# Residual quantizer on one core: norms as a ninth column, scores code by code, code constants in the mask product, a new order

## The chip, the cores and the metric

The kernel runs on one core of a Trainium2 chip. The metric is the device time of one execution in microseconds (us). A core has five engines that take their instructions in order, each from its own queue: PE (matrix products into PSUM), VectorE (DVE in the profile), ScalarE (ACT), GpSimd (POOL) and SyncE (SP), which here only issues DMAs.

## The reference

An audio codec's encoder and decoder around a residual vector quantizer, for x of shape 2 x 16000 x 512 in bf16, four codebooks of eight codes:

```python
z = sum(xp[:, i:i+T, :] * dw_enc[i] for i in range(3))   # 3 taps along time
z = silu(z)
res, q = z, 0
for s in range(4):
    cb = codebooks[s]                                     # 8 x 512
    d2 = (res*res).sum(-1)[..., None] - 2*res@cb.T + (cb*cb).sum(-1)
    idx = d2.argmin(-1)
    q, res = q + cb[idx], res - cb[idx]
y = sum(qp[:, i:i+T, :] * dw_dec[i] for i in range(3))
```

Everything is rounded to bf16 after each step, as JAX does; which code wins depends on these roundings.

## The kernel before

**Tiles.** Each of the two rows of 16000 frames is cut into tiles of G groups of 128 frames: 6, 8 and seven of 16 in the first row, seven of 16, 8 and 6 in the second, so 18 tiles, 14 of them large. A tile's frames lie so that the 512 features are four blocks of 128 partitions, with 128 frames of a group side by side.

**Stages of a tile.** `load` brings x in by transposing DMAs, one for each group, on SP. `front` makes the encoder: for each half of the features (h) three tap products of two blocks each (L538 to L541, on ScalarE or VectorE), two additions on VectorE (`TA`, `Z`), `exp` on ScalarE (L545), +1 on either (L547); `front2` the reciprocal on ScalarE (L557) and the gate product on VectorE. `select` scores three codebooks at once, `resid` subtracts the three chosen codes from z and scores the fourth, `back` multiplies the chosen codes with the decoder's taps and stores y.

**Scores.** `gram` (L561) fills PSUM for each group with 64 columns: 32 columns of z times z, block by block of 32 frames, of which a frame's own norm is the diagonal, and 32 columns of z times the 32 codes (times -2). Before these, one product of the identity with `MSK` (L569) puts -2^100 off the diagonal, so that a maximum over the 32 columns gives the norm (L609). L610 copies the code columns of three codebooks to `S` and adds `CC2`, the codes' own norms (of two codebooks; zero for the third).

**Decisions.** Then `select` takes the codebooks s = 0, 1, 2 in turn, all on arrays of 16 groups x 8 codes in each partition: the norm rounded to bf16 (`TR`), the score without the code's norm (`PR = S - CCF`, bf16), `V = PR + TR`, `KEY = V + CCB` in the upper half of a 32-bit word whose lower half holds the code's number, the minimum `M`, and the one-hot `OHA` by comparing (L370 is the helper that issues all of VectorE's two-input operations). For the next codebook, PE transposes the one-hot (L647), a copy `OT` brings it to SBUF (L652), and a product with `BD` gives the correction of the scores (L657), which L625 or L630 adds. The norm of the residual is the old one plus the chosen code's score: `E2 = RC * OHA`, its sum `RD` (L663), `rr[1] = rr[0] + RD[0]`, rounded into `TR[1]` (L666); for s = 1 `TR[2] = rr[1] + RD[1]`.

**Windows, residual, back.** `windows` transposes the one-hots by PE (L680) and copies them to `OHW` (L686), win0 for three codebooks, win3 for the fourth. `resid` has 24 pieces a tile: PE multiplies with `CBN` (L709), and the piece goes back to z by VectorE as an addition (L717) or by ScalarE as a copy, for which PE adds z itself first (L708, L715). `back` is PE (L766 to L770), a copy by ScalarE to one of four buffers `YB` (L774), and stores on SP (L797).

**What sets the order.** All steps of all tiles are recorded in a `Plan` with their engine, a cost, what they read and write, and a key. `Plan.order` then places them one after another: always the step that can start first by these costs, and among equals the one of lowest rank; the rank comes from tables (`WHEN`, by stage and by part of the run, and `NUDGE`, by stage and tile, empty here). `SHARE` and `SLACK` decide which of two engines takes a step that either can do. Where the plan leaves PE waiting over 1 us, it puts in `fill` products without a use (L817), which keep PE busy. The instructions are written out in that order, so each engine's queue is fixed.

Of the kernel before, what the change touches and what calls it, by code (L numbers as in the profile page):

```python
# [8 lines left out]
BF16 = mybir.dt.bfloat16  # L9
F32 = mybir.dt.float32  # L10
# [207 lines left out]
def kernel(  # L218
# [30 lines left out]
    SHARE = (18.22, 2.18, -1.48)  # L249
    SLACK = (0.8, -4.91, -0.79)  # L250
    QUOTA = {"ACT": 4, "DVE": 4}
    MARGIN = (0, 0, 0, 1)
    WHEN = {"setup": ((0.01, 1.859), (0.613, 1.215), (0.919, 1.13)), "load": ((-1.633, 0.741), (-1.622, 0.601), (-2.139, 0.741)),
            "pad": ((-1.343, 0.11), (-1.736, 0.115), (-2.291, 0.134)), "taps": ((0.214, 0.643), (-0.413, 0.648), (0.468, 1.172)),
            "exp": ((0.672, 0.12), (0.683, 0.024), (0.853, 0.023)), "plus1": ((1.084, 0.218), (0.349, 0.232), (0.344, 0.644)),
            "recip": ((0.542, 0.819), (0.604, 0.213), (1.49, 0.627)), "gate": ((-0.104, 0.84), (0.557, 0.649), (1.589, 0.937)),
            "score0": ((-0.134, 0.016), (0.889, 0), (0.11, 0)), "decide": ((1.83, 0.266), (-0.088, 0.293), (0.585, 0.224)),
            "win0": ((2.026, 0), (2.064, 0), (2.265, 0)), "resid": ((1.585, 0.742), (1.683, 0.632), (1.582, 0.974)),
            "score3": ((2.326, 1.043), (2.779, 0.347), (2.915, 1.644)), "decide3": ((1.265, 0.194), (2.773, 0.35), (3.38, 0.645)),
            "win3": ((3.143, 0.143), (2.987, 1.212), (3.452, 0.209)), "back": ((2.709, 0.604), (3.156, 1.105), (4.055, 0.674))}  # L260
    NUDGE = {}
# [25 lines left out]
    def sb(shape, dt, name):  # L287
# [7 lines left out]
    ONES = sb([P, P], BF16, "ONES")  # L295
    MSK = sb([P, NMK, ZW], BF16, "MSK")
    IDH = sb([P, HB, 1], F32, "IDH")
    CBT = sb([P, KT, NC], BF16, "CBT")
    CBM2 = sb([P, KT, NC], BF16, "CBM2")
    CCF = sb([P, 1, NC], F32, "CCF")  # L300
    CC2 = sb([P, 1, N3], F32, "CC2")
    CCB = sb([P, 1, NC], BF16, "CCB")
# [12 lines left out]
    SS = [{"S": sb([P, GM, N3], F32, f"S{b}"), "rr": sb([P, 3, GM, 1], F32, f"rr{b}"), "RD": sb([P, 2, GM, 1], F32, f"RD{b}"),  # L315
           "TR": sb([P, 3, GM, 1], BF16, f"TR{b}"), "RC": sb([P, GM, C], F32, f"RC{b}"), "PR": sb([P, GM, C], BF16, f"PR{b}"),
           "V": sb([P, GM, C], BF16, f"V{b}"), "M": sb([P, GM, 1], F32, f"M{b}"), "E2": sb([P, GM, C], F32, f"E2{b}"),
           "OT": [sb([GCM, P], BF16, f"OT{b}_{s}") for s in range(2)],
           "PR3": sb([P, GM, C], BF16, f"PR3{b}"), "rr3": sb([P, GM, 1], BF16, f"rr3{b}"),
           "V3": sb([P, GM, C], BF16, f"V3{b}"), "M3": sb([P, GM, 1], F32, f"M3{b}")} for b in range(2)]  # L320
# [51 lines left out]
    def setup():  # L372
# [7 lines left out]
        add("DVE", 0.25, key, lambda: nc.vector.tensor_reduce(out=IDH[:, :, 0], in_=IDENT.rearrange("p (q c) -> p c q", c=HB), axis=AX.X, op=ALU.add),  # L380
            ["I"], ["IDH"])
        add("DVE", 0.3, key, lambda: nc.vector.tensor_scalar(out=MSK[:, :, 0:HB], in0=IDH.rearrange("p c o -> p o c").to_broadcast([P, NMK, HB]),
            scalar1=BIG, scalar2=-BIG, op0=ALU.mult, op1=ALU.add), ["IDH"], ["MSK"])
# [49 lines left out]
        j = add("ACT", 0.2, key, lambda: nc.scalar.copy(CCF[:, 0, :], ps(bc)[:, 0:NC]), [], ["CCF"], after=[j])  # L433
        j = add("ACT", 0.2, key, lambda: nc.scalar.copy(CCB[:, 0, :], ps(bc)[:, 0:NC]), [], ["CCB"], after=[j])
        pool_memset(CC2, 0.0, ["CC2"], 0.2, ("setup", -5, 0))
        add("ACT", 0.2, key, lambda: nc.scalar.copy(CC2[:, 0, 0:2 * C], ps(bc)[:, 0:2 * C]), [], ["CC2"], free=bc, after=[j])

# [84 lines left out]
    def front(st, h):  # L522
# [12 lines left out]
        for k in range(K):  # L535
            for c in range(2):
                i = 2 * h + c
                dst, src, w = (tb if k else ta)[:, c], X[:, i, k:k + G, :].rearrange("p g c -> p (g c)"), WENC[:, k, i:i + 1]  # L538
                either({"ACT": act(R), "DVE": dve(R, 3.84) + 0.06}, key, lambda dst=dst, src=src, w=w: nc.scalar.mul(dst, src, w),  # L539
                       lambda dst=dst, src=src, w=w: nc.vector.tensor_scalar(out=dst, in0=src, scalar1=w, scalar2=None, op0=ALU.mult),  # L540
                       allx + ["WENC"], [("TB" if k else "TA", c)])  # L541
            if k == 1:
                tt(ta, ta, tb, ALU.add, dve(2 * R, 1.92), key, [("TB", 0), ("TB", 1)], [("TA", 0), ("TA", 1)])
        tt(Z, v(ta), v(tb), ALU.add, dve(2 * R, 1.92), key, [(t, c) for t in ("TA", "TB") for c in range(2)], zt)
# [16 lines left out]
    def gram(st, g0, g1, r0, r1, box):  # L561
        F, Z = ZF[st["n"] % NZ], ZB[st["n"] % NZ]
        for g in range(r0, r1):
# [4 lines left out]
            if u == 0:  # L568
                nc.tensor.matmul(o, lhsT=IDENT, rhs=MSK[:, 0:nb, :], start=True, stop=False)  # L569
# [8 lines left out]
    def products(st, g0, g1, key, reads, box):  # L578
        j = None
        for r0 in range(g0, g1, GPART):  # L580
            r1 = min(r0 + GPART, g1)
            j = add("PE", (r1 - r0) * 0.16 + 0.19 * (r0 == g0), key, lambda r0=r0, r1=r1: gram(st, g0, g1, r0, r1, box), reads, [],
                    take=("SA"[g1 - g0 > NMK], box) if j is None else None, dest="DVE" if j is None else None, after=[] if j is None else [j],
                    mm=(r1 - r0) * 16 + (r0 == g0))
# [5 lines left out]
    def select(st):  # L590
# [4 lines left out]
        S, M, V, PR, RC, E2 = W["S"][:, 0:G], W["M"][:, 0:G], W["V"][:, 0:G], W["PR"][:, 0:G], W["RC"][:, 0:G], W["E2"][:, 0:G]  # L595
        rr = [W["rr"][:, j, 0:G] for j in range(3)]
        TR = [W["TR"][:, j, 0:G] for j in range(3)]
        RD = [W["RD"][:, j, 0:G] for j in range(2)]
        A = OHA[n % NOH]
        zt = [("Z", n % NZ, i, u) for i in range(KT) for u in range(2)] + [("ZC", n % NZ)]  # L600
        nq = len(st["split"])
        for q, (g0, g1) in enumerate(st["split"]):
            box = {}
            key = ("score0", n, q / nq)
            j = products(st, g0, g1, key, zt + ["MSK", "I"], box)

            def evac(g0=g0, g1=g1, box=box):
                v = view(g0, g1, box)
                nc.vector.tensor_reduce(out=rr[0][:, g0:g1, 0], in_=v[:, :, 0:HB], axis=AX.X, op=ALU.max)  # L609
                nc.vector.tensor_tensor(out=S[:, g0:g1], in0=v[:, :, HB:HB + N3], in1=CC2.to_broadcast([P, g1 - g0, N3]), op=ALU.add)  # L610
            add("DVE", dve((g1 - g0) * (HB + N3)) + 0.07, key, evac, ["CC2"], [("S", b), ("rr", b, 0)], free=box, after=[j])
        small = dve(GC)
        tiny = dve(G)
        pbox = None
        for s in range(3):
            key = lambda f: ("decide", n, (s + f / 10) / 3)
            cs = slice(s * C, (s + 1) * C)
            if s == 0:
                add("DVE", tiny, key(0), lambda: nc.vector.tensor_copy(TR[0], rr[0]), [("rr", b, 0)], [("TR", b, 0)])
                tt(PR, S[:, :, cs], CCF[:, :, cs].to_broadcast([P, G, C]), ALU.subtract, small, key(0), [("S", b), "CCF"], [("PR", b)])  # L620
                rc, rct = S[:, :, cs], ("S", b)
            else:
                pc = lambda pbox=pbox: ps(pbox)[:, 0:GC].rearrange("p (g c) -> p g c", c=C)
                if s == 1:
                    add("DVE", small, key(0), lambda pc=pc, cs=cs: nc.vector.tensor_tensor(out=RC, in0=pc(), in1=S[:, :, cs], op=ALU.add),  # L625
                        [("S", b)], [("RC", b)], free=pbox, after=[pj])
                    tt(PR, RC, CCF[:, :, cs].to_broadcast([P, G, C]), ALU.subtract, small, key(0), [("RC", b), "CCF"], [("PR", b)])
                    rc, rct = RC, ("RC", b)
                else:
                    add("DVE", small, key(0), lambda pc=pc, cs=cs: nc.vector.tensor_tensor(out=PR, in0=pc(), in1=S[:, :, cs], op=ALU.add),  # L630
                        [("S", b)], [("PR", b)], free=pbox, after=[pj])
            tt(V, PR, TR[s].to_broadcast([P, G, C]), ALU.add, small, key(1), [("PR", b), ("TR", b, s)], [("V", b)])
            KY = KEY[0]
            k16 = KY.bitcast(BF16).rearrange("p g (c h) -> p g c h", h=2)
            tt(k16[:, 0:G, :, 1], V, CCB[:, :, cs].to_broadcast([P, G, C]), ALU.add, small, key(2), [("V", b), "CCB"], [("KEY", 0)])
# [26 lines left out]
            tt(E2, rc, OH, ALU.mult, small, key(5), [rct, ("OHA", n % NOH)], [("E2", b)])  # L662
            add("DVE", small, key(5), lambda s=s: nc.vector.tensor_reduce(out=RD[s][:, :, 0], in_=E2, axis=AX.X, op=ALU.add), [("E2", b)], [("RD", b, s)])  # L663
            if s == 0:
                tt(rr[1], rr[0], RD[0], ALU.add, tiny, key(6), [("RD", b, 0), ("rr", b, 0)], [("rr", b, 1)])
                add("DVE", tiny, key(6), lambda: nc.vector.tensor_copy(TR[1], rr[1]), [("rr", b, 1)], [("TR", b, 1)])  # L666
            else:
                tt(TR[2], rr[1], RD[1], ALU.add, tiny, key(6), [("RD", b, 1), ("rr", b, 1)], [("TR", b, 2)])
# [20 lines left out]
    def resid(st):  # L689
# [33 lines left out]
        PR3, rr3, V3, M3 = Q["PR3"][:, 0:G], Q["rr3"][:, 0:G], Q["V3"][:, 0:G], Q["M3"][:, 0:G]  # L723
# [131 lines left out]
```

## Time and profile before

| | |
|---|---|
| times of three runs, us | 720.34, 721.6, 722.49; median 721.6 |
| span of the profiled execution, us | 721.9 |
| mean granted PE clock, share of full | 0.956 |
| DMA, MB and mean GB/s | 71.89, 100 |
| fill products (L817) | 283, 74.3 us |
| residual pieces on VectorE (L717) | 131 |
| residual pieces on ScalarE (L715) | 301 |

The chain of work that ended last is by engine:

```profile
DVE 54%; PE 25%; ACT 9%; issue 7%; DMA 2%; SPq 1%; ACTq 0%; DVEq 0%
```

How to read the rows that follow: a group's row gives line, engine, operation, names and shapes (output <- input, partitions x elements), how often, then busy us and mean ns of one, then the engine's idle time just before and what ended it. A row of stretches gives the stretch, its length, and for each engine the busy us with the number of instructions, then the granted clock, the DMA share and GB/s. A row of waits gives who waited for whom: us in total, times, longest. A timeline row begins with start and duration in us.

### The profile page before, as it was taken

The numbers are of one execution on the slowest core, as the hardware profiler recorded it, in microseconds if no ns is written. First come the engines' busy times: TensorE is split into PE (matmuls) and PEld (weight loads), VectorE is DVE, ScalarE is ACT, GpSimd is POOL, SyncE is SP. The second block draws the span as 40 slices with busy tenths as digits, with TensorE's granted clock in tenths as the row PEclk, the third lists the DMA queues.
The fourth block names the chain that finished last, engine by engine and source line by source line (L and its number), as shares of the span: only waits on it lengthen the run. The fifth ranks groups of instructions, "written<-read, shape, count | busy, mean of one in ns | idle before, by whom it ended". The sixth has DMA issues, their size and how long they took to land.

```text
span 721.9 us, 24372 instructions
## 1 busy us (share of the span) xinstructions
PE 593.8 (82%) x10729; PEld 291.3 (40%) x10729; DVE 670.1 (93%) x1252; ACT 658.3 (91%) x581; POOL 7.0 (1%) x35
## 2 busy tenths in 40 slices
PE   5896686897788879888787988789878877899995
PEld 2343243344334434434343443334434433544442
DVE  8779799999999999999999999899999999999893
ACT  5878899799999999999999999999999999999766
POOL 2000000000000000000000000000000000000000
PEclk9999798999999999999899999999999999999998
DMA  5454464634164452535426274842544150112406
GB/s 112 102 96 97 95 119 96 139 72 88 29 164 81 111 106 87 127 66 162 90 79 129 46 155 96 158 88 77 124 143 75 38 130 31 62 60 90 143 8 213
DMA packets 163968, 71.89 MB, mean 100 GB/s; under 512 B 155567, under 2 KB 155599, under 8 KB 163862
## 3 DMA queue, kind: packets, MB, share of 16 engines
q1 hardware_dynamic: 163646, 69.90, 41.9%
q8 instruction: 84, 1.38, 0.8%
q10 hardware_dynamic: 216, 0.43, 0.2%
q14 instruction: 22, 0.18, 0.1%
HBM read 0.43 MB, written 32.77 MB: 46 GB/s over the span
## 4 chain that ended last, share of the span: by engine, by line
DVE 54%; PE 25%; ACT 9%; issue 7%; DMA 2%; SPq 1%; ACTq 0%; DVEq 0%
DVE ZB L717 12%; DVE ZB L370 10%; PE ps L709 8%; PE ps L708 6%; DVE TB L540 6%; PE ps L575 5%; DVE TA L370 4%; DVE TA L540 3%; DVE EX L547 3%; ACT EX L545 2%; DVE OHW L686 2%; ACT EX L557 2%; PE ps L766 2%; ACT ZB L715 2%; PE ps L817 2%
## 5 line engine op out<-in xcount | busy, mean ns | idle before, releaser
L709 PE MATMUL ps<-OHW,CBN 128*128 128x512 bf16 (+1 forms) x768 | 268.4, 386 | 17.6 <-DVE ZB L717 9.5
L715 ACT CAST ZB<-ps 128x1024 bf16<-128x1024 f32 (+2 forms) x301 | 257.1, 941 | 27.2 <-PE ps L709 25.0
L708 PE MATMUL ps<-ZB,IDENT 128*128 128x512 bf16 (+1 forms) x537 | 209.3, 390 | 29.0 <-DVE ZB L717 12.8
L717 DVE TENSOR_TENSOR ZB<-ZB,ps 128x1024 bf16<-128x1024 bf16 (+2 forms) x131 | 137.9, 1068 | 3.0 <-PE ps L709 2.1
L709 PEld LDWEIGHTS <-CBN 128*128 128x128 bf16 x768 | 75.3, 99 | 136.8 <-issue 69.9
L774 ACT CAST YB<-ps 128x1024 bf16<-128x1024 f32 x126 | 123.0, 1048 | 6.4 <-PE ps L766 3.9
L545 ACT ACTIVATE EX<-ZB 128x4096 bf16<-128x4096 bf16 (+2 forms) x36 | 115.0, 3198 | 11.4 <-DVE ZB L370 11.3
L557 ACT ACTIVATE EX<-EX 128x4096 bf16<-128x4096 bf16 (+2 forms) x36 | 114.6, 3195 | 0.2
L575 PEld LDWEIGHTS <-ZB 128*32 128x32 bf16 x8064 | 76.2, 96 | 51.1 <-issue 46.6
L575 PE MATMUL ps<-ZB 128*32 128x64 bf16 x8064 | 88.4, 198 | 8.3 <-DVE ZB L370 2.4
L540 DVE TENSOR_SCALAR TB<-XT,WENC 128x2048 bf16<-128x2048 bf16 (+2 forms) x135 | 90.5, 689 | 0.1
L817 PE MATMUL ps<-MSK,IDENT 128*128 128x512 bf16 x283 | 74.3, 410 | 11.0 <-issue 3.4
L766 PE MATMUL ps<-WDEC,OHW 128*128 128x512 bf16 x252 | 72.6, 382 | 12.1 <-DVE ZB L717 6.4
L708 PEld LDWEIGHTS <-IDENT 128*128 128x128 bf16 x537 | 53.9, 100 | 64.0 <-issue 12.5
L370 DVE TENSOR_TENSOR ZB<-ZB,EX 128x4096 bf16<-128x4096 bf16 (+2 forms) x36 | 72.6, 2017 | 3.6 <-ACT EX L557 3.5
L370 DVE TENSOR_TENSOR TA<-TA,TB 128x4096 bf16<-128x4096 bf16 (+2 forms) x36 | 72.7, 2019 | 1.2 <-ACT TB L539 0.8
L370 DVE TENSOR_TENSOR ZB<-TA,TB 128x4096 bf16<-128x4096 bf16 (+2 forms) x36 | 72.6, 2017 | 0.4
L540 DVE TENSOR_SCALAR TA<-XT,WENC 128x2048 bf16<-128x2048 bf16 (+2 forms) x71 | 47.4, 682 | 0.3
L817 PEld LDWEIGHTS <-IDENT 128*128 128x128 bf16 x283 | 27.7, 104 | 45.1 <-issue 21.4
L547 DVE TENSOR_SCALAR EX<-EX 128x4096 bf16<-128x4096 bf16 (+2 forms) x36 | 39.1, 1085 | 3.9 <-ACT EX L545 3.8
L766 PEld LDWEIGHTS <-OHW 128*128 128x128 bf16 x252 | 23.1, 98 | 39.5 <-issue 17.0
L686 DVE COPY OHW<-ps 96x1024 bf16<-96x1024 bf16 (+5 forms) x34 | 21.6, 635 | 10.3 <-PE ps L680 5.3
(100 smaller groups left out, 401.5 us busy)
## 6 DMA issues: line engine op xcount, KB each, us to landing
out_dram<-YB SPq DMA_DIRECT2D x33, 448.0 KB
out_dram<-YB SPq DMA_DIRECT2D x28, 512.0 KB
XT<-in_x_dram SPq DMA_TRANSPOSE x283
out_dram<-YB SPq DMA_DIRECT2D x30, 60.0 KB
out_dram<-YB SPq DMA_DIRECT2D x31, 2.0 KB
out_dram<-YB SPq DMA_DIRECT2D x2, 224.0 KB
YB<-in_dw_dec_dram ACTq DMA_DIRECT2D x1, 384.0 KB
out_dram<-YB SPq DMA_DIRECT2D x1, 384.0 KB
```

The costliest lines, as they stand in the source:

```text
L370: add("DVE", cost, key, lambda: nc.vector.tensor_tensor(out=out, in0=a, in1=b, op=op), reads, writes, **kw)
L540: lambda dst=dst, src=src, w=w: nc.vector.tensor_scalar(out=dst, in0=src, scalar1=w, scalar2=None, op0=ALU.mult),
L545: add("ACT", act(2 * R), ("exp", n, h), lambda: nc.scalar.activation(v(ex), Z, ACT.Exp, scale=-1.0), zt, [("EX", sl), "ACTTAB"], hold="E")
L557: nc.scalar.add_instruction(mybir.InstActivation(name=nc.get_next_instruction_name(), engine=mybir.EngineType.Activation, func=ACT.Reciprocal,
L575: nc.tensor.matmul(o[HB * q:HB * (q + 1), u * ZW:(u + 1) * ZW].rearrange("p (s c) -> p s c", s=2), lhsT=blk, rhs=both, start=False, stop=( ...
L708: nc.tensor.matmul(o, lhsT=IDENT, rhs=zg[:, k0:k0 + nk, :], start=True, stop=False)
L709: nc.tensor.matmul(o, lhsT=CBN[s, u][:, i * P:(i + 1) * P], rhs=W[:, k0:k0 + nk, PADC:PADC + P], start=not on_act, stop=True)
L715: nc.scalar.copy(zg, v)
L717: nc.vector.tensor_tensor(out=zg, in0=zg, in1=v, op=ALU.add)
L766: nc.tensor.matmul(o, lhsT=W[:, k, PADC:PADC + P], rhs=WDEC[u], start=True, stop=not wrap)
L774: add("ACT", act_psum(1024), key, lambda k=k, box=box, Y=Y, k0=k0: nc.scalar.copy(Y[:, 2 * (k - k0):2 * (k - k0) + 2, :].rearrange("p g d ...
L817: nc.tensor.matmul(PS[j // 2][:, 512 * (j % 2):512 * (j % 2) + NMK * ZW], lhsT=IDENT, rhs=MSK.rearrange("p u w -> p (u w)"), start=True, s ...
```

## The change

Four edits.

1. The frame's norm is kept as a ninth column of `E2`, beside the eight masked scores, so that one sum over nine columns gives the next norm; the separate `rr`, `RD` and their addition go.
2. `PR`, `V`, `TR`, `PR3`, `V3`, `rr3` and the constants are laid out code by code (codes outermost, groups innermost), `S`, `RC` and `KEY` group by group as before.
3. `MSK` has three more rows, in which the code norms of two codebooks stand as three bf16 parts; `TID` (32 rows of identity, three rows of ones) takes the identity's place in the mask product, which so adds the code norms. `CC2` goes, and L610's addition is a copy. The mask has 35 rows in place of 128. The fill product multiplies ones (`FB`) in place of `MSK`.
4. The tables `SHARE`, `SLACK`, `WHEN` have other numbers, and `NUDGE` has 17 rows of 18 numbers, one for each tile.

```diff
-    SHARE = (18.22, 2.18, -1.48)
-    SLACK = (0.8, -4.91, -0.79)
+    SHARE = (94.853, 2.191, 1.099)
+    SLACK = (-12.996, -111.301, -17.404)
...
-    NUDGE = {}
+    NUDGE = {"back": (3.954, -1.84, 0.016, 0.025, 0.009, 0.557, 0.035, -0.021, 0.035, 0.051, 0.006, 0.002, 0, 0.181, 0.022, 0.443, 3.888, 2.204),
...
-        add("DVE", 0.25, key, lambda: nc.vector.tensor_reduce(out=IDH[:, :, 0], in_=IDENT.rearrange("p (q c) -> p c q", c=HB), axis=AX.X, op=ALU.add),
-            ["I"], ["IDH"])
...
+        idh = IDENT[0:HB, 0:HB].rearrange("p (o c) -> p o c", o=1)
+        add("DVE", 0.2, key, lambda: nc.vector.tensor_copy(TID[0:HB], idh.to_broadcast([HB, P // HB, HB])), ["I"], ["TID"])
...
-        pool_memset(CC2, 0.0, ["CC2"], 0.2, ("setup", -5, 0))
-        add("ACT", 0.2, key, lambda: nc.scalar.copy(CC2[:, 0, 0:2 * C], ps(bc)[:, 0:2 * C]), [], ["CC2"], free=bc, after=[j])
...
+        def ccrows():
+            for q in range(NPART):
+                nc.tensor.matmul(ps(bq)[0:2 * HB, 0:NC], lhsT=EQ[:, q, :], rhs=CCD[:, q, :], start=(q == 0), stop=(q == NPART - 1))
+        j = add("PE", 0.4, key, ccrows, ["CCD", "EQ"], [], take=("S", bq), mm=NPART)
+        add("DVE", 0.2, key, lambda: nc.vector.tensor_copy(MSK[HB:KM, :, HB:HB + 2 * C], ps(bq)[HB:KM, 0:2 * C].rearrange(
+            "p (o c) -> p o c", o=1).to_broadcast([KM - HB, NMK, 2 * C])), [], ["MSK"], free=bq, after=[j])
...
-                nc.tensor.matmul(o, lhsT=IDENT, rhs=MSK[:, 0:nb, :], start=True, stop=False)
+                nc.tensor.matmul(o, lhsT=TID.rearrange("p q c -> p (q c)"), rhs=MSK[:, 0:nb, :], start=True, stop=False)
...
-                nc.vector.tensor_reduce(out=rr[0][:, g0:g1, 0], in_=v[:, :, 0:HB], axis=AX.X, op=ALU.max)
-                nc.vector.tensor_tensor(out=S[:, g0:g1], in0=v[:, :, HB:HB + N3], in1=CC2.to_broadcast([P, g1 - g0, N3]), op=ALU.add)
+                nc.vector.tensor_reduce(out=E2[0][:, g0:g1, C], in_=v[:, :, 0:HB], axis=AX.X, op=ALU.max)
+                nc.vector.tensor_copy(S[:, g0:g1], v[:, :, HB:HB + N3])
...
-                tt(PR, S[:, :, cs], CCF[:, :, cs].to_broadcast([P, G, C]), ALU.subtract, small, key(0), [("S", b), "CCF"], [("PR", b)])
+                tt(PR, swap(rc), CCF[:, cs].to_broadcast([P, C, G]), ALU.subtract, small, key(0), [rct, "CCF"], [("PR", b)])
...
-            tt(V, PR, TR[s].to_broadcast([P, G, C]), ALU.add, small, key(1), [("PR", b), ("TR", b, s)], [("V", b)])
+            tt(V, PR, TR[s].to_broadcast([P, C, G]), ALU.add, dve(GC, 1.92), key(1), [("PR", b), tr(s)], [("V", b)])
...
-            tt(k16[:, 0:G, :, 1], V, CCB[:, :, cs].to_broadcast([P, G, C]), ALU.add, small, key(2), [("V", b), "CCB"], [("KEY", 0)])
+            tt(swap(k16[:, 0:G, :, 1]), V, CCB[:, cs].to_broadcast([P, C, G]), ALU.add, small, key(2), [("V", b), "CCB"], [("KEY", 0)])
...
-            tt(E2, rc, OH, ALU.mult, small, key(5), [rct, ("OHA", n % NOH)], [("E2", b)])
-            add("DVE", small, key(5), lambda s=s: nc.vector.tensor_reduce(out=RD[s][:, :, 0], in_=E2, axis=AX.X, op=ALU.add), [("E2", b)], [("RD", b, s)])
-            if s == 0:
-                tt(rr[1], rr[0], RD[0], ALU.add, tiny, key(6), [("RD", b, 0), ("rr", b, 0)], [("rr", b, 1)])
-                add("DVE", tiny, key(6), lambda: nc.vector.tensor_copy(TR[1], rr[1]), [("rr", b, 1)], [("TR", b, 1)])
-            else:
-                tt(TR[2], rr[1], RD[1], ALU.add, tiny, key(6), [("RD", b, 1), ("rr", b, 1)], [("TR", b, 2)])
+            tt(E2[s][:, :, 0:C], rc, OH, ALU.mult, small, key(5), [rct, ("OHA", n % NOH)], [e2(s)])
+            res = E2[1][:, :, C] if s == 0 else W["RR"][:, 0:G]
+            add("DVE", dve(G * (C + 1)), key(5), lambda s=s, res=res: nc.vector.tensor_reduce(out=res, in_=E2[s], axis=AX.X, op=ALU.add),
+                [e2(s)], [e2(1) if s == 0 else ("RR", b)])
+            if s == 1:
+                add("DVE", tiny, key(6), lambda: nc.vector.tensor_copy(TR[2][:, 0, :], W["RR"][:, 0:G]), [("RR", b)], [tr(2)])
...
-                nc.vector.tensor_copy(PR3[:, g0:g1], v[:, :, HB + N3:])
+                nc.vector.tensor_copy(PR3[:, :, g0:g1], swap(v[:, :, HB + N3:]))
...
-            nc.tensor.matmul(PS[j // 2][:, 512 * (j % 2):512 * (j % 2) + NMK * ZW], lhsT=IDENT, rhs=MSK.rearrange("p u w -> p (u w)"),
-                             start=True, stop=True)
+            nc.tensor.matmul(PS[j // 2][:, 512 * (j % 2):512 * (j % 2 + 1)], lhsT=IDENT, rhs=FB, start=True, stop=True)
```

`swap` exchanges groups and codes in an access pattern; it moves nothing.

## The prediction

> **What bounds the kernel now.** I read the busy shares first, then the span in four stretches, then the waits, then the prices of single operations.
>
> ```profile
> PE 593.8 (82%) x10729; PEld 291.3 (40%) x10729; DVE 670.1 (93%) x1252; ACT 658.3 (91%) x581; POOL 7.0 (1%) x35
> ```
> ```profile
> core 0: us, PE busy (x) PEld busy (x) DVE busy (x) ACT busy (x) POOL busy (x), PEclk, DMA share, GB/s
> 0.00:60.00 60.00, 47.45 (x525) 22.29 (x526) 48.34 (x151) 44.49 (x79) 3.78 (x29) 0.94 0.49 102
> 60.00:144.00 84.00, 61.24 (x885) 28.00 (x884) 77.93 (x120) 72.90 (x55) 0.00 (x0) 0.86 0.53 110
> 144.00:648.00 504.00, 422.54 (x8207) 210.75 (x8205) 485.98 (x844) 486.93 (x387) 3.18 (x6) 0.97 0.42 95
> 648.00:722.00 74.00, 62.53 (x1117) 30.26 (x1114) 57.82 (x140) 53.93 (x62) 0.00 (x0) 0.96 0.33 114
> ```
>
> In the middle, 144 to 648 us, VectorE and ScalarE are both over 96% busy (18.0 and 17.1 us idle of 504): one microsecond of VectorE work less is there nearly a microsecond of span less, if ScalarE's idle time can shrink with it. At the two ends VectorE is idle for 11.7 of the first 60 us and 16.2 of the last 74, so work put there can be hidden. VectorE's waits in the middle add up to 15.9 us; these are the longest:
>
> ```profile
> DVE OHW L686 <- PE ps L575: 3.9, 3, 2.0
> DVE rr L609 <- PE ps L575: 2.7, 5, 1.0
> DVE ZB L717 <- PE ps L709: 1.8, 4, 0.9
> ```
>
> Prices next: VectorE's groups with shapes kept apart (mean ns of one after the comma), and a stretch of its timeline (start, us).
>
> ```profile
> L370 DVE TENSOR_TENSOR TA<-TA,TB 128x4096 bf16<-128x4096 bf16 x28 | 64.0, 2285 | 0.3
> L370 DVE TENSOR_TENSOR TA<-TA,TB 128x2048 bf16<-128x2048 bf16 x4 | 4.9, 1223 | 0.9 <-ACT TB L539 0.8
> L370 DVE TENSOR_TENSOR V<-PR,TR 128x128 bf16<-128x128 bf16 x42 | 12.3, 293 | 0.1
> L610 DVE TENSOR_TENSOR S<-ps,CC 128x192 f32<-128x192 f32 x30 | 10.4, 346 | 0.0
> L418 DVE COPY GR<-ps 32x32 f32<-32x32 f32 x1 | 0.2, 179 | 0.6 <-PE ps L462 0.6
> L734 DVE CAST PR<-ps 128x64 bf16<-128x64 f32 x30 | 6.4, 212 | 0.0
> L440 DVE TENSOR_REDUCE GD<-IDENT 128x16 f32<-128x128 bf16 x1 | 0.3, 267 | 0.0
> L380 DVE TENSOR_REDUCE IDH<-IDENT 128x32 f32<-128x128 bf16 x1 | 0.2, 243 | 0.0
> ```
> ```profile
> 660.10 0.28 DVE L370 TENSOR_TENSOR V<-PR,rr 128x128 bf16<-128x128 bf16 x1
> 660.30 0.22 DVE L370 TENSOR_TENSOR E<-RC,OHA 128x64 f32<-128x64 f32 x1
> 660.44 0.29 DVE L370 TENSOR_TENSOR KEY<-V,CCB 128x128 bf16<-128x128 bf16 x1
> 660.64 0.21 DVE L663 TENSOR_REDUCE RD<-E 128x8 f32<-128x64 f32 x1
> ```
>
> Neighbours overlap: a listed 280 ns operation holds the engine for 0.20 us (660.10 to 660.30), a 64-element one for 0.14. So I price by start-to-start times: 0.20 − 0.135 over 64 elements is 1.05 ns an element; a tiny operation (`rr` 310.23 to 310.31 in the timeline) is 0.08. The long bf16 additions run at (2285 − 1223) / 2048 = 0.52 ns an element.
>
> **The change, part by part.**
>
> *Scores code by code.* `V = PR + TR` now has the 16 groups innermost, so both bf16 inputs and the output step by one element; before, `TR` stood still in the inner loop. Value: 0.52 ns in place of 1.05, 128 × 0.53 = 68 ns each, four per tile of 16 groups. Bounds: 0 (it stays at 293 ns, as `V` is now) and 68; I take 68, since the long additions are the same operation on the same types.
>
> *Norm as ninth column.* The additions `rr[1] = rr[0] + RD` go: 18 × 0.08 = 1.4 us. Two reductions a tile read 9 columns in place of 8: 16 × 1.05 = 17 ns each. The other addition becomes a cast of the same length: nothing.
>
> Together a large tile saves 4 × 68 + 80 − 2 × 17 = 318 ns; 14 of them 4.45 us, the four small ones 0.7.
>
> *Constants by the mask product.* L610's addition from PSUM becomes a copy. From 32 to 64 elements copies from PSUM in f32 go from 179 to 212 ns, 1.03 an element, so 192 elements give 212 + 128 × 1.03 = 344: no gain on 346. Bounds: 0, or half the element time, 30 × 0.1 = 3 us; I take 0. The mask product itself has the same 512 columns; PE has 82 us to spare in the middle. Setup loses `CC2` and `IDH` and gains three small matmuls, two small VectorE operations and some 1 us of POOL memsets (MSK's 128x512 took 0.52), ahead of the pad copies; these stood 3.9 us waiting for their DMA, which covers it. Without that cover the first taps would be 1 us late.
>
> *Long steps.* Codes outermost make some reads and writes jump: `PR` from `S` (96 bytes), from `RC` (32), from PSUM; `KEY` is written at every 32 bytes. The nearest row is L380, which reads 128 elements 64 bytes apart in 243 ns, no slower than L440's 128 neighbours in 267. I take 0. For PSUM no row has such steps: 128 + 2 × 64 elements a tile, at most one element time more, 14 × 256 × 1.05 = +3.8 us; low end 0.
> The Trainium skill (SBUF — State Buffer, Door 1: The DMA port swizzle, its note on cachelines) says the opposite of L380: a step that leaves a 16-byte line at each element pays a penalty, with no figure. By that rule the sum below would be a loss, by the row it is unchanged; the row is of this chip and this engine, and decides.
>
> *Order chosen anew.* Counting the built programs against each other: in the large tiles the 336 residual pieces are split 100 on VectorE, 236 on ScalarE in both. What moves lies in the ends and the small tiles. ScalarE loses six of ten tap products (12.3 to 4.4 us at its rows of 0.93, 1.14 and 2.05), three CBN products (2.15) and nine 128x512 pieces, and gains eight 128x384 pieces, one +1 and one window copy: about −9 us. VectorE gains six tap products (2 × 0.67 + 0.40 + 3 × 0.33 = 2.7), CBN (0.8) and on balance 1.7 of residual pieces, less 0.8 for the +1 and the window copy: +4.4. With −5.2 from above VectorE's total stays (670 to 669), but its work leaves the full middle for the ends.
>  - *Middle:* −4.45 by arithmetic. For the waits: the cover that VectorE's queue holds between writing the one-hot and taking its transpose back, and from there to the correction product, falls short of 1 us by 9.4 us in all before and 11.5 after, so +2.1 at worst; the win0 copies are covered better (short of 1.3 us by 2.6, now 1.3); PE fills from the fifth tile on fall from 70 to 19, 51 × 0.262 = 13 us of waits no longer filled. Ends: +2.1 and −15.9 (all waits gone). Nearest is the L686 row, three waits with 3.9 us; I take half of it, −2.0.
>  - *Start:* waits on ScalarE (3.5 + 2.2 + 0.8 us, first 144 us) could go, the added taps could all stand on the path: −3.9 to +2.6. VectorE does the first half's taps before it builds `DJ`; on the other side the second reciprocal is queued behind two tap products of 1.1 us. I take −0.5.
>  - *End:* tile 17's residual was 19 pieces of 0.47 us on VectorE against 5 on ScalarE and is now 11 to 13, 3.8 us less; tile 16's goes the other way, 12 to 21 pieces, +1.7 on balance. I take −1.0. The last 8 us (three last products, ScalarE's copies, the store's landing) are the same.
>  - *SP's queue* has the same 283 loads and the same stores, some loads now ahead of stores. In the middle no VectorE wait is on a load, and stores already stood 229 us waiting for `YB`; a store that comes later holds the loads behind it, and the taps after those.
>
> Sum: 721.9 − 4.45 − 2.0 − 0.5 − 1.0 = 713.9. The median shown is 721.6, 0.3 below the profiled execution's span: 713.6.
>
> **The rivals.**
>  - *The order removes most waits.* For it: the fills. −4.45, three quarters of 15.9 (19/70 left) −11.6, ends −3: 702.6. Against: the decide chain's cover isn't better.
>  - *Only the arithmetic arrives,* or the change's packing does not take place: 721.6 − 4.45 = 717.2; with `V` left at 293 ns (14 × 4 × 68 ns back) 721.0. For it: cover as before.
>  - *Slower, by the clock.* 58 of 283 fills go, 51 of them where PE is idle a sixth of the time. From 60 to 144 us the granted clock is 0.86 and VectorE idles 7.2%, in the middle 0.97 and 3.6%. If the middle fell to that state, 3.6% of 504 = +18 us: 713.6 + 18 = 732. It decides from about 8 us on, near a clock of 0.92. Against: in the middle PE is 84% busy, and the stretch at 0.86 holds the most fills.
>  - *Slower, by the long steps.* 1024 elements a tile (3 × 128 reads, 4 × 128 writes, 2 × 64 from PSUM) at one element time more: 14 × 1024 × 1.05 = 15 us: 728.7. It decides from 0.56 ns an element. Against: L380.
>
> **How the numbers follow.** Forecast 0.56 (own range 708 to 719.5), most waits gone 0.14, only arithmetic 0.15, clock 0.08, long steps 0.07. A measurement tells about 0.3% from no change, 719.4 to 723.8. Faster: 0.53 + 0.14 + 0.10 = 0.77; same: 0.03 + 0.05 + 0.01 = 0.09; slower 0.14. The range runs from the waits case, 702, to 722; the slower cases and little else lie outside.
>
> **What would show it.** `V` at about 226 ns, the copy to `S` near 344, `KEY` and `PR` below 300; 360 and more for `KEY` means the long steps cost. VectorE near 669 us, ScalarE near 649; in the middle VectorE's idle at 14 to 18 us. The forecast is wrong if VectorE's waits in the middle exceed 22 us or the granted clock there falls below 0.93, and too timid if they are under 8.

## The result, and the profile after

The changed kernel takes 745.28 us (median of four runs, 744.62 to 747.24) against 721.81 for the kernel before beside it: ratio 1.0339, interval 1.0323 to 1.0355. The forecast was 713.6 with a range of 702 to 722; the change makes the kernel 3.4% slower.

The page of the changed kernel (its profiled execution: time 744.8, span 742.7), busy shares, then its middle stretch, 144 to 648 us:

```profile
PE 583.3 (79%) x10610; PEld 288.3 (39%) x10673; DVE 694.9 (94%) x1243; ACT 650.3 (88%) x572; POOL 8.1 (1%) x40
```
```profile
144.00:648.00 504.00, 402.28 (x7902) 202.12 (x7931) 492.14 (x803) 470.28 (x364) 3.17 (x6) 0.95 0.42 93
```

VectorE's busy time rose by 24.8 us (670.1 to 694.9), the span by 20.8, the median by 23.5. In the middle VectorE is now idle for only 11.9 of 504 us, and ScalarE for 33.7 in place of 17.1: VectorE alone is the bound, and it has more to do. The granted clock there is 0.95. So this is no new wait, it is work. The groups of VectorE, shapes kept apart, say which; first two rows of the kernel before, then the changed kernel:

```profile
L370 DVE TENSOR_TENSOR KEY<-V,CCB 128x128 bf16<-128x128 bf16 x56 | 16.4, 296 | 0.0
L370 DVE TENSOR_TENSOR PR<-S,CCF 128x128 bf16<-128x128 f32 x14 | 4.0, 283 | 0.0
```
```profile
L387 DVE TENSOR_TENSOR KEY<-V,CCB 128x128 bf16<-128x128 bf16 x56 | 38.5, 714 | 0.1
L387 DVE TENSOR_TENSOR PR<-S,CCF 128x128 bf16<-128x128 f32 x14 | 6.4, 460 | 0.0
L660 DVE TENSOR_TENSOR PR<-ps,S 128x128 bf16<-128x128 f32 x14 | 6.4, 457 | 0.0
L387 DVE TENSOR_TENSOR PR<-RC,CCF 128x128 bf16<-128x128 f32 x14 | 5.6, 400 | 0.1
L387 DVE TENSOR_TENSOR V<-PR,TR 128x128 bf16<-128x128 bf16 x42 | 9.3, 221 | 0.0
L641 DVE COPY S<-ps 128x192 f32<-128x192 f32 x30 | 10.4, 346 | 0.0
L762 DVE CAST PR<-ps 128x64 bf16<-128x64 f32 x30 | 6.3, 211 | 0.0
```

`V` fell from 293 to 221 ns, as forecast (226), and the copy to `S` stands at 346 (344 was expected). But `KEY`, written at every 32 bytes, went from 296 to 714 ns, and `PR`, which reads floats at every 96 or 32 bytes, from 283 to 460 and 400. L660, `PR` for the third codebook, reads `S` at every 96 bytes and also PSUM at every 32; it takes 457 (284 before), no more than with `S` alone. `PR3`'s cast is L762: it reads PSUM at every 256 bytes and costs what it cost before (211 against 212). The fourth decision's `V`, not among the rows, went only from 282 to 267.

### The profile page after: what moved, and what is told of

The parts are those of the page before. It is cut to its first block, busy times and chain, and to the rows that moved or that the text cites. A ratio compares the mean times of both kernels' runs of the same rounds, so it can differ in the third digit from the quotient of the medians.

```text
span 742.7 us, 24185 instructions
## 1 busy us (share of the span) xinstructions
PE 583.3 (79%) x10610; PEld 288.3 (39%) x10673; DVE 694.9 (94%) x1243; ACT 650.3 (88%) x572; POOL 8.1 (1%) x40
## 4 chain that ended last, share of the span: by engine, by line
DVE 64%; PE 25%; issue 7%; ACT 3%; DMA 1%; DVEq 0%; ACTq 0%; SPq 0%
DVE ZB L387 12%; DVE ZB L744 12%; DVE TB L569 7%; PE ps L736 5%; DVE KEY L387 4%; PE ps L845 4%; PE ps L605 4%; DVE TA L387 4%; PE ps L735 4%; DVE TA L569 4%; DVE EX L577 3%; PE ps L794 2%; DVE OHW L713 2%; DVE OHA L387 1%; ACT YB L802 1%
## 5 line engine op out<-in xcount | busy, mean ns | idle before, releaser
L735 PE MATMUL ps<-ZB,IDENT 128*128 128x512 bf16 (+1 forms) x536 | 205.2, 383 | 27.5 <-DVE ZB L744 15.1
L744 DVE TENSOR_TENSOR ZB<-ZB,ps 128x1024 bf16<-128x1024 bf16 (+2 forms) x132 | 141.0, 1088 | 1.1 <-PE ps L736 0.7
L605 PEld LDWEIGHTS <-ZB 128*32 128x32 bf16 x8064 | 77.0, 96 | 50.2 <-issue 48.4
L569 DVE TENSOR_SCALAR TB<-XT,WENC 128x2048 bf16<-128x2048 bf16 (+2 forms) x140 | 94.4, 690 | 0.2
L794 PE MATMUL ps<-WDEC,OHW 128*128 128x512 bf16 x212 | 68.6, 402 | 16.4 <-DVE ZB L744 9.0
L735 PEld LDWEIGHTS <-IDENT 128*128 128x128 bf16 x536 | 53.1, 99 | 62.5 <-issue 8.6
L845 PE MATMUL ps<-FB,IDENT 128*128 128x512 bf16 x207 | 59.7, 429 | 22.3 <-DVE S L641 7.3
L569 DVE TENSOR_SCALAR TA<-XT,WENC 128x2048 bf16<-128x2048 bf16 (+2 forms) x72 | 48.5, 688 | 0.4 <-DMA XT<-in_x_dram 0.2
L387 DVE TENSOR_TENSOR KEY<-V,CCB 128x128 bf16<-128x128 bf16 (+2 forms) x72 | 44.8, 643 | 0.3
L845 PEld LDWEIGHTS <-IDENT 128*128 128x128 bf16 x225 | 23.3, 106 | 52.7 <-issue 35.0
```

What stands on the lines that cost most here:

```text
L387: add("DVE", cost, key, lambda: nc.vector.tensor_tensor(out=out, in0=a, in1=b, op=op), reads, writes, **kw)
L605: nc.tensor.matmul(o[HB * q:HB * (q + 1), u * ZW:(u + 1) * ZW].rearrange("p (s c) -> p s c", s=2), lhsT=blk, rhs=both, start=False, stop=( ...
L735: nc.tensor.matmul(o, lhsT=IDENT, rhs=zg[:, k0:k0 + nk, :], start=True, stop=False)
L744: nc.vector.tensor_tensor(out=zg, in0=zg, in1=v, op=ALU.add)
L794: nc.tensor.matmul(o, lhsT=W[:, k, PADC:PADC + P], rhs=WDEC[u], start=True, stop=not wrap)
L845: nc.tensor.matmul(PS[j // 2][:, 512 * (j % 2):512 * (j % 2 + 1)], lhsT=IDENT, rhs=FB, start=True, stop=True)
```

## The experiments

All times are medians, beside runs of the kernel before on the same chip; ratios are to those, with their intervals.

**The layout, taken out in two steps.** e1 writes the keys group by group again and lets that addition read `V` at every 32 bytes instead:

```diff
-            tt(swap(k16[:, 0:G, :, 1]), V, CCB[:, cs].to_broadcast([P, C, G]), ALU.add, small, key(2), [("V", b), "CCB"], [("KEY", 0)])
+            tt(k16[:, 0:G, :, 1], V.rearrange("p c g -> p g c"), CCB[:, cs].rearrange("p c o -> p o c").to_broadcast([P, G, C]), ALU.add, small, key(2), [("V", b), "CCB"], [("KEY", 0)])
```

> The changed kernel with one edit: KEY is written group by group again (a step of 4 bytes), and V is read with the long step instead. Theory (long steps cost, the write of KEY most: it went from 296 to 714 ns for 128 elements, 72 of them): KEY falls to 300 if only long writes cost, to about 460 if a long read of V costs as PR's reads of S and RC do (400 to 460 ns); VectorE's busy time falls from 695 by 14 to 24 us and the time from 745.3 to between 723 and 733. Rival (the new order costs the time, VectorE's extra work stands in idle time): the time stays within 5 us of 745.

e2 lays out `PR`, `V`, `TR`, `PR3`, `V3`, `rr3` and the constants group by group, as before the change; ninth column, mask constants, tables and with them the order on every queue are the changed kernel's:

```diff
-                tt(PR, swap(rc), CCF[:, cs].to_broadcast([P, C, G]), ALU.subtract, small, key(0), [rct, "CCF"], [("PR", b)])
+                tt(PR, rc, CCF[:, :, cs].to_broadcast([P, G, C]), ALU.subtract, small, key(0), [rct, "CCF"], [("PR", b)])
...
-            tt(V, PR, TR[s].to_broadcast([P, C, G]), ALU.add, dve(GC, 1.92), key(1), [("PR", b), tr(s)], [("V", b)])
+            tt(V, PR, TR[s].to_broadcast([P, G, C]), ALU.add, dve(GC, 1.92), key(1), [("PR", b), tr(s)], [("V", b)])
```

> The changed kernel with the layout of PR, V, TR, KEY, PR3, V3, rr3 and the constants group by group as before; the ninth column, the mask's constants and the new order stay, instruction for instruction. Theory (long steps are all of the loss): VectorE's busy time 670 us or a little more (745's 694.9 - 26 for KEY - 7 for PR + 5 for V at 293 ns), time between 712 and 721. Rival (the order): the time stays above 735.

e2's group of `KEY`:

```profile
L387 DVE TENSOR_TENSOR KEY<-V,CCB 128x128 bf16<-128x128 bf16 x56 | 16.3, 297 | 0.1
```

Measured: e1 732.42 (ratio 1.0142, 1.0104 to 1.0181), VectorE 680.5, `KEY` 381 ns, between the two values expected; e2 724.87 (1.0033, 1.001 to 1.0056), 4 us above the range expected, VectorE 673.1, `KEY` 297, `PR` 284 to 315, `V` 284. From the changed kernel to e1 VectorE loses 14.4 us and the time 12.9; from e1 to e2 7.4 and 7.5. The layout by codes therefore costs 745.28 − 724.87 = 20.4 us, nearly all of the loss, `V`'s gain already taken off it. What is left of the change without it is 3.6 us slower than before (721.24 beside it). The forecast for that rest was 4.1 us faster: 8, less the 3.8 that `V` was to save.

**Which distance costs.** e9 adds VectorE instructions to the kernel before, behind its last one, on tiles no longer in use: additions of 128 elements a partition with a step on one side, three of each kind.

```diff
+        st_ = lambda t, k: t[:, 0:128 * k].rearrange("p (n k) -> p n k", k=k)[:, :, 0]
+        one = lambda o, a, c: nc.vector.tensor_tensor(out=o, in0=a, in1=c, op=ALU.add)
+        for _ in range(3): one(st_(U16O, 16), st_(A16, 1), st_(B16, 1))
```

> The kernel before with VectorE instructions added behind its last one, three of each kind, on tiles no longer in use: additions of 128 elements a partition in which one side has a step. Theory (the distance from one element to the next is what costs, and from 16 bytes on): two-byte results written every 2 to 8 bytes about 300 ns, every 16, 32 and 64 bytes about 700; float reads every 4 and 8 bytes about 300, every 16 to 64 bytes 400 to 460; two-byte reads every 16 to 64 bytes about 380; the copy that reads floats every 64 bytes about 243 as in row L380. Rival (the loss comes from the pattern of two short loops in the changed kernel, not from the distance): all of them lie near 300 and the copies near 240.

The profile of e9 in stretches that hold one kind each (stretch, its length, VectorE's busy us with the number of instructions, then clock, DMA share, GB/s). Six kinds of two-byte results, written every 2, 4, 8, 16, 32 and 64 bytes:

```profile
709.03:709.81 0.78, 0.68 (x3) 1.00 0.08 29
709.81:710.83 1.02, 0.92 (x3) 1.00 0.08 30
710.83:712.27 1.44, 1.33 (x3) 1.00 0.99 310
712.27:714.55 2.28, 2.18 (x3) 0.94 0.83 257
714.55:716.73 2.18, 2.08 (x3) 0.50 0.85 269
716.73:718.97 2.24, 2.14 (x3) 0.50 0.11 40
```

and floats read every 8, 16 and 32 bytes:

```profile
725.65:726.63 0.98, 0.88 (x3) 0.50 0.04 8
726.63:727.86 1.23, 1.13 (x3) 0.50 0.00 0
727.86:729.11 1.25, 1.15 (x3) 0.50 0.00 0
```

A third of each is one instruction: two-byte writes 227, 307, 443, 727, 693, 713 ns, reads 293, 377, 383. Written floats (291 and 294 at 4 and 8 bytes, 373 to 388 from 16 on) and two-byte reads (293, then 366 to 382) rise like the float reads, by some 75 to 95 ns in 128 elements, 0.6 to 0.7 ns each. Two-byte results are a case of their own: at 8 bytes they cost 1.1 ns an element more than at 4, at 16 and beyond (727 − 307) / 128 = 3.3. The theory holds for the distance, and misses three prices: two-byte writes rise from 8 bytes on, the float reads stay below 400, and the copies are not free. The writes at 8 to 32 bytes ran while the DMA engines were 83 to 99% busy, but at 64 bytes, with 11%, the cost is that at 32. The rival, that the pattern of two loops and not the distance costs, falls for the write: these are plain steps. A copy is hit least: reading floats it takes 227 ns at 4 bytes, 274 at 32 and 272 at 64.

e7 keeps e2's memory layout and has the two key writers take the elements in another sequence: in the select steps two codes of one group, then the next group 32 bytes on; in the last decision four codes, which are 16 bytes.

```diff
-            tt(k16[:, 0:G, :, 1], V, CCB[:, :, cs].to_broadcast([P, G, C]), ALU.add, small, key(2), [("V", b), "CCB"], [("KEY", 0)])
+            tt(lo(k16[:, 0:G, :, 1], 2), lo(V, 2), cb4(cs, 2, G), ALU.add, small, key(2), [("V", b), "CCB"], [("KEY", 0)])
...
-        tt(k16[:, 0:G, :, 1], V3, CCB[:, :, cs].to_broadcast([P, G, C]), ALU.add, small, key, [("V3", b), "CCB"], [("KEY", 1)])
+        tt(lo(k16[:, 0:G, :, 1], 4), lo(V3, 4), cb4(cs, 4, G), ALU.add, small, key, [("V3", b), "CCB"], [("KEY", 1)])
```

> The group layout with the new order; the two writers of the keys take the same elements in another sequence: in the select steps two codes (4 bytes apart) and then the next group 32 bytes on; in the last decision four codes (16 bytes in all), then the next group. If each element that starts another stretch of 16 bytes costs extra: select's keys about (297+714)/2 = 505 ns if each jump costs as in the changed kernel (half the elements jump), the last decision's about 297 + 417/4 = 400 ns. If instead only the sequence's innermost step counts, both stay at 297. If any split sequence is slow, both are near 714.

A stretch of e7 with one key of each kind (minimum, median, maximum in ns):

```profile
L387 DVE TENSOR_TENSOR KEY<-V,CCB x2: 292/358/424, 317.9 to 318.1; 128x128 bf16<-128x128 bf16 x2
```

The last decision's key takes 292, no more than in the plain sequence, the select step's 424; 400 and 505 were expected if each jump costs. No theory had this pair. With e9 it reads so: four two-byte writes to one stretch of 16 bytes cost no more than the plain sequence, two (here, and at 8-byte steps: 443) cost a third of the full penalty, one costs all of it.

**The order, alone.** e3 is the changed kernel with the old tables, e4 is e2 with the old tables:

```diff
-    SHARE = (94.853, 2.191, 1.099)
-    SLACK = (-12.996, -111.301, -17.404)
+    SHARE = (18.22, 2.18, -1.48)
+    SLACK = (0.8, -4.91, -0.79)
...
+    NUDGE = {}
```

> The changed kernel with the old tables SHARE, SLACK, WHEN and an empty NUDGE: the layout code by code in the old order. Theory (long steps): KEY again near 700 ns, time between 740 and 752. Rival (the order): near 722.

> Layout group by group and the old tables: what is left of the change is the ninth column, the mask's constants, the fills of ones and the setup. Both theories: VectorE 1 us less than before, time 719 to 724. Against the run with the new order and the same layout it shows what the new order is worth by itself: the forecast had 3.5 us for it.

Measured 766.15 (ratio 1.0607) and 748.68 (1.0366): 20.9 and 23.8 us above the same steps in the new order. e4's VectorE is busy for 682.0 of 748.8 us, 67 idle. Both lie far above what was expected. So the old tables are no neutral setting: with them the order is planned anew for a changed list of steps, and these two runs don't tell what the new order is worth against the old one. Why that order comes out so much slower was not followed up.

**The start.** In the changed kernel three copies on VectorE are slow, while GpSimd fills the low halves of the keys. Timelines of VectorE and then GpSimd, changed kernel (start, us):

```profile
6.21 1.28 DVE L472 COPY SEL<-IDENT 32x128 bf16<-32x128 bf16 x2
6.41 1.11 DVE L487 COPY ROW<-IDENT 32x128 bf16<-32x128 bf16 x1
```
```profile
6.38 1.02 POOL L377 MEMSET KEY<- 128x16 uint16 x14
```

The two copies of `SEL` and that of `ROW` took 172 and 175 ns each before, 1211 and 1112 here; all three end at 7.5 us, just after the last fill at 7.4. In e5, which is e2 with the fills of `FB`, `TID` and `EQ` written ahead of GpSimd's first pad copy, the keys are done 1.2 us sooner:

```diff
+    def early():
+        nc.gpsimd.memset(FB, 1.0)
+        nc.gpsimd.memset(TID[HB:KM], 1.0)
+        nc.gpsimd.memset(EQ, 0.0)
...
+            if not begun and s["k"][0] == "pad" and s["c"] == 1.0:
+                begun = True
+                early()
```

> The kernel laid out group by group with the new order, and GpSimd's fills of the filler data, the identity rows and the selector written ahead of its first copy of a pad column instead of behind it, so that the sixteen fills of the keys end about 1.2 us sooner. Everything else is in the same order on every queue. Theory (VectorE's three copies at 6 to 7 us wait for GpSimd's fills): the selector copies fall from 1174 ns towards 270, the row copy from 1075 towards 180, the first exponential starts about 1 us earlier and the time falls from 724.9 to about 723.9. Rival (the start is set by the products for the decoder's weights or by the loads): the copies get short and the time stays at 724.9 (within 0.3).

e5's timeline of VectorE:

```profile
6.36 0.27 DVE L472 COPY SEL<-IDENT 32x128 bf16<-32x128 bf16 x2
```

The copies are short again (174 and 176 ns), and the time is 723.03 (1.0015, 0.9998 to 1.0033): by the medians 1.8 us below e2, where 1 was expected; the two intervals overlap, so the size is rough.

**The arithmetic without the layout.** e8 is e5 with the norm `TR` written twice side by side, so that `V` reads pairs and each bf16 input steps by one element; nothing is moved by 32 bytes. e6 puts the same pairs, and the ninth column, into the kernel before with its own order; the row addition is left out and nothing else moves. In both, only the first three decisions of a tile read pairs; the fourth keeps its addition as it was (281 ns).

```diff
-            tt(V, PR, TR[s].to_broadcast([P, G, C]), ALU.add, small, key(1), [("PR", b), ("TR", b, s)], [("V", b)])
+            tt(pr(V), pr(PR), TR[s].rearrange("p g (o h) -> p g o h", o=1).to_broadcast([P, G, C // 2, 2]), ALU.add, small, key(1), [("PR", b), ("TR", b, s)], [("V", b)])
```

> The kernel before with its own layout and its own order, and only two parts of the change's idea: the row part is written twice side by side, so that V's addition reads all its inputs with a step of one element without any long step, and the ninth column takes the place of the row addition (which is left out of the queue; nothing else moves). Theory (the arithmetic is worth what the forecast gave it, and it was the layout by codes that cost): V 293 to about 225 ns, 54 of them about -3.4 us, row additions -1.4, reductions +0.5: VectorE about 666 us instead of 670 and the time about 717.2. Rival (the old order fits the old durations, as the run of the old order with the new steps was slower than either): V gets as short, and the time is 720 to 723.

> The run with GpSimd's fills early, and the row part written twice side by side so that V's addition runs at the doubled rate without long steps. Theory (in the middle a us of VectorE's work is a us of time): V 284 to about 222 ns, VectorE -3.2 us, time 3.2 us below the run with the early fills alone, about 720.7. Rival (waits take it back): less than 1 us below that run.

e6's group of `V`:

```profile
L370 DVE TENSOR_TENSOR V<-PR,TR 128x128 bf16<-128x128 bf16 x42 | 9.1, 216 | 0.1
```

e6 takes 717.37 (ratio 0.9933, 0.9906 to 0.996) with VectorE at 665.2: 4.3 us faster than before where 4.5 were expected, and the only version that beats it. e8 takes 721.43 (0.9991, 0.997 to 1.0011), 1.6 below e5 with VectorE 3.3 lower: half the theory's 3.2, with intervals that overlap too.

**Where the new order's gain went.** Of the new tables' moves, ten steps in the first 70 us go from ScalarE to VectorE: three `CBN` products and seven tap products of the first three tiles. e10 is e8 with these ten back on ScalarE, e11 is e6 with the same ten moved to VectorE; every other step keeps its place. The edit in e10 (e11 names `DVE`):

```diff
+            if s["n"] in moved:
+                s["box"]["dest"] = "ACT"
```

> The run with early fills and paired row part (median 721.4, VectorE 669.2), with the ten steps of the first 70 us that the new tables had given to VectorE back on ScalarE, where the old tables had them: three CBN products, five tap products of the first tile and the second, two of the third (listed together about 4.6 us of VectorE). All other steps stay where they are. Theory (time is VectorE's busy time plus about 52, wherever in the run the work lies): VectorE about 665.5, time about 718. Rival (at the start VectorE has idle time, 11.7 of the first 60 us, so work moved there is hidden): the time stays within 1 us of 721.4, or grows because ScalarE takes twice as long for each.

> The reverse: the kernel before with the paired row part and the ninth column (median 717.4, VectorE 665.2), with the same ten early steps moved from ScalarE to VectorE. Theory: VectorE about 669, time about 721. Rival (hidden in VectorE's idle time at the start): 717 to 718, or less because the first exponentials come sooner.

e11 takes 721.28 (0.9988, 0.9966 to 1.0011): 3.9 us more than e6, with VectorE 3.7 busier (668.9). The theory holds there and the rival, that VectorE's idle time at the start hides such work, falls. The kept profiles show where the time goes. These are ScalarE's first and tenth exponentials in e6, then in e11 (in brackets ScalarE's idle time just before, waiting for VectorE's `Z`):

```profile
18.10 1.48 ACT L545 ACTIVATE EX<-ZB 128x1536 bf16<-128x1536 bf16 x1 [1.46 <-DVE ZB L370]
129.12 3.62 ACT L545 ACTIVATE EX<-ZB 128x4096 bf16<-128x4096 bf16 x1 [4.68 <-DVE ZB L370]
```
```profile
19.59 1.48 ACT L545 ACTIVATE EX<-ZB 128x1536 bf16<-128x1536 bf16 x1 [6.52 <-DVE ZB L370]
133.52 3.62 ACT L545 ACTIVATE EX<-ZB 128x4096 bf16<-128x4096 bf16 x1 [4.68 <-DVE ZB L370]
```

e11 is 1.5 us late at the first, 4.4 at the tenth and still 4.6 at the last (645.62 and 650.26). In the first 144 us ScalarE waits 9.4 us for `Z` before exponentials in e6 and 23.5 in e11.

e10 missed: 725.12 (1.0048, 1.0026 to 1.007), 3.7 slower than e8 although VectorE is 2.9 less busy. Two of its waits in the first 144 us:

```profile
DVE RC L657 <- PE ps L687: 3.4, 1, 3.4
DVE ZB L387 <- ACT TB L568: 2.3, 2, 1.8
```

The second is new (VectorE waits for a tap product now on ScalarE), the first was 2.2 in e8. Together VectorE's waits there rise from 15.6 to 21.1 us. Here, an order planned with these steps on one engine did not become better with them on the other.

**The kernel before, again.** c0 is the kernel before unchanged.

> The kernel before once more, for a profile nearer its median than the one shown at first (whose span of 721.9 lay above it). Both theories expect a span of 718 to 720 and the time VectorE sits idle, span less busy time, of about 49 us, as in the changed versions (46.9 to 48.9). If before has 52 us of idle again, the new order has taken some 3 us of waiting away and given them back in VectorE's busy time.

The run came out at 725.43 (span 723.6, VectorE 669.8), higher than its usual median, so it gives no profile near the median either; it was expected to have a span of 718 to 720, and its 54 us of idle time decide as little as the 52 of the first profile.

**All versions in one table.** Time is about 2 us more than the span in each run that shows both (744.8 and 742.7, 716.0 and 714.1). So the last column, VectorE's idle time at the median, is median − 2 − busy, with the busy time of the one profiled execution.

| version | median, us | VectorE busy, us | idle at the median, us |
|---|---|---|---|
| before | 721.7 | 670.1 | 49.6 |
| changed | 745.3 | 694.9 | 48.4 |
| e1 | 732.4 | 680.5 | 49.9 |
| e2 | 724.9 | 673.1 | 49.8 |
| e5 | 723.0 | 672.5 | 48.5 |
| e8 | 721.4 | 669.2 | 50.2 |
| e6 | 717.4 | 665.2 | 50.2 |
| e11 | 721.3 | 668.9 | 50.4 |
| e10 | 725.1 | 666.3 | 56.8 |
| e3 | 766.2 | 703.9 | 60.3 |
| e4 | 748.7 | 682.0 | 64.7 |

In eight of the eleven the idle time is 48.4 to 50.4 us, and the time is VectorE's busy time plus about 51.5: these versions differ in what VectorE has to do. e3, e4 and e10 fall out, two with the tables set back and one with steps moved. e11, in which the same steps were moved the other way, does not, so this is a description of these runs and no rule for when an order fits.

## Why the prediction was wrong

**The step that failed: "Long steps … I take 0".** It rested on one row, L380. That row is a reduction that reads, and the term held kinds that it doesn't show: four keys a tile that write two bytes at every 32 (+418 ns listed each), and additions that read floats at 32 and 96 bytes (+117 and +177). Among the steps tested alone even the same reading, two bytes at every 64, costs an addition 73 ns more (293 to 366), and a copy is hit least (47 ns at 32 bytes). No run tests a reduction, so why L380 showed no loss stays open. In place of 0 the layout measured +20.4 us, after `V`'s gain. The rule of the Trainium skill (SBUF — State Buffer, Door 1: The DMA port swizzle, its note on cachelines), which the prediction set aside for the row, was right in kind: by it, two accesses to a 16-byte line suffice for full speed. For reads e9 agrees at the steps tried: 293 ns at 8 bytes, 377 at 16. For two-byte writes the measurement differs from the page: two to a line cost 443 (e9) or 424 (e7), and only with four (e7's 292) was there no loss.

**The rival for it was right in mechanism and too small.** It came to 728.7, with one element time more for each long step. Measured, the reads cost 0.6 to 1.4 ns an element more, the PSUM reads nothing that shows, and the key's writes list 3.3: half of the rival's elements carried three times its price.

**What was right.** `V` at the doubled rate: 221 ns (226 expected), and as pairs without long steps 216. The copy in place of L610's addition: 346, no gain. The arithmetic as a whole: −4.45 forecast, −4.3 measured in e6, though by pairs and not by the layout, and with three of a tile's four `V`; so the agreement is partly luck. (The prediction's 1.05 ns an element is 1.02 by the two times it gives, 0.20 and 0.135; that takes 0.2 us off.) VectorE's total without the long steps and ScalarE's: 669 and 649 forecast, 669.2 and 648.5 in e8. Fewer waits in the middle: VectorE's waits there fell from 15.9 us before to 9.7 in the changed kernel, and its idle time from 18.0 to 11.9 (e6 16.3, e8 12.0), more than the −2.0 allowed. The clock rival did not come: 0.95 in the middle, above the 0.92 from which it decides.

**The second wrong step: "its work leaves the full middle for the ends", with the start at −0.5.** The idea that VectorE's idle time in the first 60 us can hide added work is false: e11 put 3.7 us there and got 3.9 back as time, with the delay in place by the tenth exponential. The bound given for the start (+2.6) held the tap products alone; the `CBN` products were left out of it. The start is a chain: ScalarE's exponentials wait for VectorE's `Z` (9.4 us in e6, 23.5 in e11), and work put on VectorE ahead of `Z` lengthens that wait.

The terms for the middle, the start and the end together, −3.5 in the forecast, came out as a loss: e8, with order and mask constants, is 4.1 us slower than e6. In its profile VectorE is 4.0 us busier than in e6, near the +4.4 that the forecast had counted but let the ends hide, and over the whole span just as idle, 48.9 us. What it idles less in the middle it idles more at the end. From the last exponential to the end of the span (VectorE alone), e6 and then e8:

```profile
645.62:714.10 68.48, 52.39 (x127) 0.97 0.35 119
```
```profile
649.33:718.10 68.77, 49.36 (x123) 0.98 0.39 134
```

VectorE has 3.0 us less to do there and the stretch is no shorter (68.81 us in the kernel before); the forecast had −1.0. VectorE's waits after 648 us are 5.4 us in e6 and 9.1 in e8, all of them for PE. So here the forecast's picture is turned round: work left the end, where that bought no time, and was done earlier. No run takes the start and the end of the new order apart.

**A third, small: "3.9 us waiting for their DMA, which covers it"** for GpSimd's added fills. The cover was there, but the plan put the fills of `FB`, `TID` and `EQ` behind the pad copy, not ahead of it, and so pushed the keys' fills onto VectorE's copies: about 1.8 us by the medians of e2 and e5.

Together: +20.4 for the layout, where −3.8 was forecast, and +3.1 to +3.6 for the rest, where −4.1 was forecast.

## What to carry to other kernels

Before choosing a layout for the sake of a doubled rate, price every instruction that has to cross it: here one two-byte write per 16 bytes listed 3.3 ns an element more (some 2.5 of it on VectorE's path, as the next section shows), against the 0.56 that the packed addition saved (293 to 221 ns). Where the reason for the layout is one operand that stands still, write that operand twice side by side instead; this keeps all steps short and gave 216 ns. On a kernel with one saturated engine, count its busy time over the whole run, ends included, and believe that idle time at an end hides work only after a run: at this start it did not.

## What was not expected of the hardware

A slow write is not held to its full listed length. In the changed kernel's timeline of VectorE the next instruction starts 0.31 us after the key, and takes longer in turn:

```profile
316.08 0.70 DVE L387 TENSOR_TENSOR KEY<-V,CCB 128x128 bf16<-128x128 bf16 x1
316.39 2.50 DVE L387 TENSOR_TENSOR TA<-TA,TB 128x4096 bf16<-128x4096 bf16 x1
```

In e2, between 144 and 648 us, the next instruction starts 0.20 us after a key in the same places, and this addition lists 2.28 or 2.29. So a slow key costs 0.11 + 0.21, some 0.32 us on the path, for 0.42 listed. The same holds there for nearly all keys with an instruction behind them that doesn't need the key: it starts 0.31 to 0.33 us after, and mostly lists about 0.2 more. That is why the listed sums (56 keys by 417 ns alone are 23.4 us) exceed VectorE's growth of 21.8 us for the whole layout, and why the fourth decision's `V`, often right behind a slow key, lists 267 ns on average and 219 in e1.

The float reads in the kernel cost more than e9's plain steps: 400 ns against 383 at 32 bytes, and 460 at 96, a step that e9 doesn't have, against 367 at 64. That wasn't tried further.
